# Three x tiles transposed by DMA instead of TensorE at the end of block 0, with one load and four small loads moved to other queues

## The chip, the cores and the metric

The kernel runs on one core of one Trainium2 chip. The metric is device time in microseconds (us), lower is better. The core's engines run side by side, each through its own list of instructions in program order: PE (TensorE, matrix products; its weight loads are shown apart as PEld), DVE (VectorE), ACT (ScalarE), POOL (GpSimd) and SP (SyncE). SP computes nothing here: it issues DMAs, and a DMA that it issues waits behind whatever SP issued before. All DMAs run on the core's 16 DMA engines. In the profile q1 is the queue of SP's DMAs and q0 that of the DMAs which POOL issues.

## What is computed

A linear attention with position weights, and behind it a gated feed-forward layer on its output. Cut to what matters:

```python
# q, k, v: (8 batches, 8 heads, 576 rows, 64) f32
phi(x) = concat([relu(x) * cos_w, relu(x) * sin_w], axis=-1)     # 64 -> 128
kv  = einsum('bhsf,bhsd->bhfd', phi(k), v);  z = sum_s phi(k)
out = einsum('bhsf,bhfd->bhsd', phi(q), kv) / (einsum('bhsf,bhf->bhs', phi(q), z) + 1e-6)
x   = out.transpose(0, 2, 1, 3).reshape(8 * 576, 512)
xn  = x / sqrt(mean(x * x, -1) + 1e-6) * rms_g
g   = xn @ w_gate                                                # 512 -> 1536
y   = (g * sigmoid(g) * (xn @ w_val)) @ w_out                    # 1536 -> 512
```

## The kernel before

The 4608 rows are worked in nine blocks of 512: blocks 0 to 7 are the first 512 rows of each batch, block 8 holds the last 64 rows of all eight batches (the tails). Blocks run in the order 0, 1, 2, 3, 4, 5, 6, 8, 7. A block has 12 steps of gate and value products (`gval_step`: four matmuls of 128x512 into a bank psG, four into a bank psV; then ACT makes the Silu of psG and DVE multiplies it with psV), and four steps of output products (`out_mm`, 12 matmuls each). psG and psV have two banks each, used in turn.

While PE works on block b, the attention of batch b+1 is made in its shadow. The order is written out by hand: `at(block, step, where, f, ...)` puts a call into a slot of a step, and the place of the call in the program is its place on each engine that it uses. In block 0 the steps 12 to 15 are pieces of the output products (`out_first`), with slots "pe", "mid", "pre" and "post". The pieces that matter here:

- `load_k`, `load_v`, `load_q` of a batch: 1 to 1.15 MB each from HBM into a ring of five tiles (`raw`). The loads of batch 2 are issued by POOL (G in the code) in the slots 8, 10 and 11 of block 0 (lines 714, 717 and 720); those of the later batches by SP.
- `q_phi` (DVE makes the cosine half, ACT the sine half) turns a quarter of a batch's q into bf16. For batch 2 the four quarters stand in steps 1 to 4 of block 1. Each is then transposed by a DMA of SP (`q_tr_dma`, line 320, tile qpT). The products with kv (`nd_pe`, line 417) read qpT: for batch 2 quarter 0 in step 6 of block 1, the others in steps 8, 10 and 12.
- `nd_post` and `x_sq` divide and square a tile of 128 rows of x; POOL makes the power -1/2 (line 488, `rs`); `x_norm` on DVE makes the bf16 tile `xn` (line 495).
- A tile `xn` (128 rows, 512 columns) is transposed into `xnT`, from which the matmuls of its block read. There are two ways. `x_tr` has PE make four transposes of 128x128 into a bank psV (line 514), and ACT (even tiles) or DVE (odd tiles) copies the bank to xnT (lines 277 and 279). `x_tr_dma` has SP issue one DMA that transposes the tile from one place of the on-chip memory to another (line 508). Before the change batch 1 uses `x_tr` for all four tiles, batches 2 to 7 use `x_tr_dma`.
- The first matmul of block 1 (line 524) needs all four tiles of batch 1.
- `load_q_tails` loads the last 64 rows of q of two batches by two DMAs of 128 KB (tile rqt, line 134), issued by SP. They are read in step 3 of a later block: the pair of batches 2 and 3 in block 2, the pair of batches 0 and 1 in block 3.
- The outputs of block 0 are copied from the banks by ACT and DVE (`osb`) and stored by four DMAs of SP (line 558).

`X1` names, for each of the four x tiles of batch 1, the slot of its products, of its norm and of its transposition:

```python
    X1 = (
        ((12, "mid"), (13, "pe"), (14, "pe")),
        ((13, "pe"), (13, "mid"), (14, "mid")),
        ((13, "mid"), (14, "pe"), (15, "pe")),
        ((14, "pe"), (14, "mid"), (15, "mid")),
    )
```

Of the kernel before, what the change touches and what calls it, by code (L numbers as in the profile page):

```python
# [17 lines left out]
def kernel(  # L18
# [11 lines left out]
    nc = tc.nc  # L30
# [16 lines left out]
    V, A, G = nc.vector, nc.scalar, nc.gpsimd  # L47
# [12 lines left out]
    psV = [ps.tile([P, 512], FP32, name=f"psV{i}") for i in range(2)]  # L60
# [67 lines left out]

    rqt = {}

    def load_q_tails(pair):
        rqt[pair] = two.tile([P, H, D], FP32, name="rqt", tag="rqt")
        for i in range(2):
            nc.sync.dma_start(
                out=rqt[pair][64 * i : 64 * i + 64, :, :],
                in_=q[2 * pair + i, :, 512:576, :].rearrange("h s d -> s h d"),
            )
# [558 lines left out]
    def at(blk, n, where, f, *args):  # L696
        slots.setdefault((blk, n), {}).setdefault(where, []).append((f, args))
# [19 lines left out]
    at(0, 10, "post", load_kv, "v", 2, (0, HP), G)  # L717
    at(0, 12, "pe", kvz_pe, 1)
    at(0, 12, "pe", kvz_evac, A, 1)
    at(0, 11, "post", load_q, 2, (0, 4), G)  # L720

    def x_tr(b, j, bank):
        x_tr_pe(b, j, bank)
# [3 lines left out]
# [6 lines that stand above are left out]
# [3 lines left out]
        if j:  # L736
            at(0, *X1[j - 1][1], x_norm, 1, j - 1)
    at(0, *X1[3][1], x_norm, 1, 3)
    for j in range(4):
        at(0, *X1[j][2], x_tr, 1, j, psV[j % 2])  # L740
    for nb in range(2, B):
        b = nb - 1
        first = nb == 2
# [24 lines left out]
    for pair in range(4):  # L768
        b = 2 * pair or 3
        if pair == 0:  # L770
            at(1, 15, "post", load_q_tails, 0)
        at(b, 3, "post", q_tails_phi, V, pair, 0)
        at(b, 3, "post", q_tails_phi, A, pair, 1)
        at(b, 3, "post", q_tails_tr_dma, pair)
        at(b, 12, "pe", nd_tails_pe, pair)
        at(b, 12, "pre", nd_post, 2 * pair + 1, 4)
        at(b, 12, "post", x_sq, 2 * pair + 1, 4)
        at(b, 13, "post", x_norm, 2 * pair + 1, 4)
        at(b, 13, "post", x_tr_dma, 2 * pair + 1, 4)
    for nb in range(3, B):  # L780
        b = nb - 2
        late = b == 1
        at(b, 0, "post", load_kv, "k", nb)
        at(b, 5 if late else 3, "post", load_kv, "v", nb)
        at(b, 8 if late else 6, "post", load_q, nb)
        if nb % 2 == 1:
            at(b, 9, "post", load_q_tails, nb // 2)

    def gval_step(blk, n):
        run(blk, n, "pe")  # L790
# [86 lines left out]
```

## Time and profile before

| what | value |
|---|---|
| median of 3 runs | 325.4 us (324.87 to 326.1) |
| the profiled execution | 325.76 us, of which the span from first to last instruction is 324.0 us |
| PE busy | 317.4 us (98% of the span) |
| PEld, DVE, ACT, POOL busy | 163.7, 184.3, 165.2, 40.7 us |
| granted TensorE clock | 1.000 over the span |
| DMA | 53.37 MB, 165 GB/s mean; q1 57.0% and q0 16.5% of 16 engines' span |
| SP's x transposes (line 508, 24 of them for xnT) | 1.19 / 1.22 / 3.83 us to issue (least, median, most) |

Times inside the span are counted from its start. A row of the timeline has the start, the length, the engine, the line and operation, the output and input, and, in brackets, the idle time before it with what ended it. Matmul ends are modelled: the distance from one start to the next tells what a matmul costs on PE, here 0.216 us for one of 512 columns. "us to landing" is the time from a DMA's issue until its data are there.

### The profile page before, as it was taken

What the parts mean: (1) busy time and instruction counts of PE and PEld (TensorE: products, weight loads), DVE (VectorE), ACT (ScalarE), POOL (GpSimd) and SP (SyncE); (2) the same over time, 40 slices, a digit from 0 to 9 for tenths busy, and PEclk for the clock granted to TensorE, in tenths of its full rate; (3) what the DMA queues carried; (4) which work ended last, traced back from release to release, by engine and by line L of the source; (5) the groups of instructions that cost most, each with busy time, mean ns of one, the idle gap of its engine ahead of it and who ended that gap; (6) DMA issues with size and microseconds to landing.
All of it is one profiled execution on the core that took longest, in us unless ns stands there. A gap on an engine that the chain in (4) does not pass through costs nothing.

```text
span 324.0 us, 6128 instructions
## 1 busy us (share of the span) xinstructions
PE 317.4 (98%) x2348; PEld 163.7 (51%) x2348; DVE 184.3 (57%) x379; ACT 165.2 (51%) x319; POOL 40.7 (13%) x78
## 2 busy tenths in 40 slices
PE   7989999999999999999999999999999999999996
PEld 3679665544454445444454445444544444444444
DVE  7784858757727774576557745782577034204410
ACT  5664856754574547445754575446643343223321
POOL 9771212001000110011001000110011000000000
PEclk9999999999999999999999999999999999999999
DMA  7999995999579966998699958995822300041002
GB/s 228 231 266 273 281 327 212 228 204 259 125 178 216 231 193 159 200 229 210 171 205 214 211 149 182 223 200 144 134 49 41 123 32 0 2 98 32 2 32 97
DMA packets 77627, 53.37 MB, mean 165 GB/s; under 512 B 50410, under 2 KB 71326, under 8 KB 77598
## 3 DMA queue, kind: packets, MB, share of 16 engines
q1 hardware_dynamic: 70374, 39.81, 57.0%
q0 software_dynamic: 7216, 13.17, 16.5%
q8 instruction: 18, 0.29, 0.4%
q14 instruction: 11, 0.09, 0.1%
q10 hardware_dynamic: 8, 0.00, 0.0%
HBM read 37.83 MB, written 9.44 MB: 146 GB/s over the span
## 4 chain that ended last, share of the span: by engine, by line
PE 92%; DMA 5%; POOL 2%; issue 0%; DVE 0%; POOLq 0%
PE psC L547 27%; PE psG L524 27%; PE psV L524 27%; DMA wv<-in_moe_w_val_dram 5%; PE psA L417 2%; PE psG L547 2%; PE psA L361 2%; PE psV L611 2%; PE psG L611 1%; PE psA L368 1%; POOL raw L124 1%; PE psA L442 0%; POOL wg L174 0%; POOL vv L204 0%; PE psC L337 0%; PE psV L514 0%
## 5 line engine op out<-in xcount | busy, mean ns | idle before, releaser
L544 DVE TENSOR_TENSOR hT<-psV,sg 128x512 bf16<-128x512 f32 x100 | 68.9, 689 | 102.2 <-PE psV L524 65.9
L543 ACT ACTIVATE sg<-psG 128x512 f32<-128x512 f32 x100 | 59.2, 592 | 63.2 <-PE psG L524 63.2
L524 PE MATMUL psV<-xnT,wv 128*128 128x512 bf16 x352 | 90.3, 379 | 0.0
L524 PE MATMUL psG<-xnT,wg 128*128 128x512 bf16 x352 | 90.3, 379 | 0.0
L547 PE MATMUL psC<-wo,hT 128*128 128x512 bf16 (+1 forms) x408 | 89.1, 376 | 0.0
L547 PEld LDWEIGHTS <-hT 128*128 128x128 bf16 x456 | 42.8, 98 | 47.1
L524 PEld LDWEIGHTS <-wv 128*128 128x128 bf16 x400 | 39.1, 98 | 47.2
L524 PEld LDWEIGHTS <-wg 128*128 128x128 bf16 x400 | 37.1, 98 | 39.7
L488 POOL TENSOR_TENSOR rs<-ms,mhalf 128x1 f32<-128x1 f32 x36 | 19.8, 551 | 195.9 <-ACT scr L483 195.9
L277 ACT COPY osb<-psC 128x512 f32<-128x512 f32 x32 | 18.8, 586 | 50.0 <-PE psC L547 50.0
L483 ACT ACTIVATE scr<-xt 128x513 bf16<-128x513 f32 x36 | 22.8, 634 | 24.5 <-DVE xt L467 24.5
L495 DVE SCALAR_TENSOR_TENSOR xn<-xt,rs,gb 128x512 bf16<-128x512 f32 (+1 forms) x37 | 26.9, 730 | 9.7 <-POOL rs L488 9.7
L283 ACT ACTIVATE kp<-raw,tab 128x256 bf16<-128x256 f32 (+2 forms) x50 | 28.4, 609 | 2.5 <-DMA raw<-in_k_dram 2.5
L467 DVE TENSOR_TENSOR xt<-psA,rec 128x512 f32<-128x512 f32 x36 | 24.9, 691 | 1.2
L283 ACT ACTIVATE qp<-raw,tab 128x512 bf16<-128x512 f32 x32 | 22.6, 713 | 1.1 <-DMA raw<-in_q_dram 1.0
L285 DVE TENSOR_SCALAR kp<-raw,tab 128x256 bf16<-128x256 f32 (+2 forms) x54 | 20.3, 421 | 0.7 <-DMA raw<-in_k_dram 0.7
L285 DVE TENSOR_SCALAR qp<-raw,tab 128x512 bf16<-128x512 f32 x31 | 15.3, 498 | 1.6 <-DMA raw<-in_q_dram 1.6
L417 PEld LDWEIGHTS <-qpT 128*128 128x128 bf16 x224 | 10.5, 97 | 6.6 <-issue 0.5
L524 PE MATMUL psG<-xnT_tail,wg 128*128 128x512 bf16 x48 | 12.3, 379 | 0.0
L524 PE MATMUL psV<-xnT_tail,wv 128*128 128x512 bf16 x48 | 12.3, 379 | 0.0
L417 PE MATMUL psA<-kvzs,qpT 128*128 128x65 bf16 x224 | 11.4, 193 | 0.0
L279 DVE CAST vv<-raw 116x1280 bf16<-116x1280 f32 (+1 forms) x13 | 10.5, 805 | 0.0
(95 smaller groups left out, 181.0 us busy)
## 6 DMA issues: line engine op xcount, KB each, us to landing
out_dram<-osb SPq DMA_DIRECT2D x31, 256.0 KB, 2.4
raw<-in_k_dram SPq DMA_DIRECT2D x5, 1120.0 KB, 8.1
raw<-in_v_dram SPq DMA_DIRECT2D x5, 1120.0 KB, 7.7
raw<-in_q_dram SPq DMA_DIRECT2D x5, 1024.0 KB, 9.0
raw<-in_k_dram POOLq DMA_DIRECT2D x2, 1152.0 KB, 19.5
raw<-in_v_dram POOLq DMA_DIRECT2D x2, 1152.0 KB, 15.9
raw<-in_q_dram POOLq DMA_DIRECT2D x2, 1024.0 KB, 16.0
wg<-in_moe_w_gate_dram POOLq DMA_DIRECT2D x3, 512.0 KB, 14.7
```

Of the source, the lines that this page charges most:

```text
L277: A.copy(out=o, in_=i)
L283: A.activation(out=out_ap, in_=in_ap, func=AF.Relu, scale=scale)
L285: eng.tensor_scalar(out=out_ap, in0=in_ap, scalar1=scale, scalar2=0.0, op0=ALU.mult, op1=ALU.max)
L417: nc.tensor.matmul(heads[:, g, hp, :], lhsT=qpT[:, h, j * P : (j + 1) * P], rhs=kvzs[b][:, g, hp * E : (hp + 1) * E], start=True, stop=True,)
L467: V.tensor_tensor(out=xt[:, 0:DM].rearrange("p (hp g d) -> p g hp d", g=2, d=D), in0=heads[:, :, :, 0:D], in1=rec[:, :, :].unsqueeze(3).to ...
L483: A.activation(out=scr[:, :], in_=xt[:, 0 : DM + 1], func=AF.Square, scale=1.0 / math.sqrt(DM), accum_out=ms[:, :],)
L488: G.tensor_tensor(out=rs[:, :], in0=ms[:, :], in1=mhalf[:, :], op=ALU.pow)
L495: V.scalar_tensor_tensor(out=xn_of[(b, j)][:, c], in0=x_of[(b, j)][:, c], scalar=rs_of[(b, j)][:, :], in1=gb[:, c], op0=ALU.mult, op1=ALU. ...
L524: nc.tensor.matmul(bank[:, cols[0] : cols[1]], lhsT=w[:, t, n * P : (n + 1) * P], rhs=x[:, t, cols[0] : cols[1]], start=(t == 0), stop=(t ...
L543: A.activation(out=sg[:, :], in_=g[:, 0:TB], func=AF.Silu)
L544: V.tensor_tensor(out=hT[:, n, :], in0=v[:, 0:TB], in1=sg[:, :], op=ALU.mult)
L547: nc.tensor.matmul(bank[:, 0 : cols[1] - cols[0]], lhsT=hT[:, n, j * P : (j + 1) * P], rhs=wo[:, n, cols[0] : cols[1]], start=(n == 0), st ...
```

## The change

In block 0, the tiles 0, 1 and 2 of batch 1 are transposed by `x_tr_dma` instead of `x_tr`, in the slot of their norm (one step earlier than before); tile 3 stays on PE and its copy on DVE. The load of q of batch 2 leaves POOL and slot (0, 11) and goes to SP, behind the three transposes, in slot (0, 14). `load_q_tails` gets the issuing engine as an argument: the pair of batches 0 and 1 and the pair of batches 2 and 3 are now loaded by POOL, in the same slots as before; the other two pairs stay with SP.

```diff
-    def load_q_tails(pair):
+    def load_q_tails(pair, eng=nc.sync):
         rqt[pair] = two.tile([P, H, D], FP32, name="rqt", tag="rqt")
         for i in range(2):
-            nc.sync.dma_start(
+            eng.dma_start(
...
-    at(0, 11, "post", load_q, 2, (0, 4), G)
...
-    for j in range(4):
-        at(0, *X1[j][2], x_tr, 1, j, psV[j % 2])
+    for j in range(3):
+        at(0, *X1[j][1], x_tr_dma, 1, j)
+    at(0, *X1[3][2], x_tr, 1, 3, psV[1])
+    at(0, *X1[3][1], load_q, 2)
...
-            at(1, 15, "post", load_q_tails, 0)
+            at(1, 15, "post", load_q_tails, 0, G)
...
-            at(b, 9, "post", load_q_tails, nb // 2)
+            at(b, 9, "post", load_q_tails, nb // 2, G if nb == 3 else nc.sync)
```

SP's list after its first two loads was: four stores of block 0, the two DMAs of k of batch 3, four transposes of q of batch 2. It becomes: three transposes of x, q of batch 2, the four stores, k of batch 3, the four transposes of q.

## The prediction

> **What bounds the kernel now.** I read the chain of waits first. Its share by engine, and three of its pieces around the changed place (start, length, engine, bank and line, matmuls):
>
> ```profile
> PE 92%; DMA 5%; POOL 2%; issue 0%; DVE 0%; POOLq 0%
> ...
> 54.23 0.86 PE psG L547 x4
> 55.75 1.29 PE psC L547 x6
> 57.04 0.86 PE psG L524 x4
> ```
>
> The DMA's 5% is one wait, for a weight that lands at 24.4 us. From there the pieces of PE follow each other to the end: the kernel is bound by PE's list of matmuls. So a change pays only by what it takes off that list, and costs only where PE has to wait. Next, PE's own timeline where the removed transposes stand:
>
> ```profile
> 52.33 0.39 PE L514 MATMUL psV<-ident,xn 128*128 128x128 bf16 x4
> 52.55 0.59 PE L547 MATMUL psC<-wo,hT 128*128 128x512 bf16 x2
> 52.98 1.03 PE L547 MATMUL psG<-wo,hT 128*128 128x512 bf16 x4
> 53.84 0.39 PE L514 MATMUL psV<-ident,xn 128*128 128x128 bf16 x4
> 54.07 1.03 PE L547 MATMUL psG<-wo,hT 128*128 128x512 bf16 x4
> 54.93 0.59 PE L547 MATMUL psC<-wo,hT 128*128 128x512 bf16 x2
> 55.36 0.39 PE L514 MATMUL psV<-ident,xn 128*128 128x128 bf16 x4
> 55.59 1.46 PE L547 MATMUL psC<-wo,hT 128*128 128x512 bf16 x6
> 56.88 0.59 PE L524 MATMUL psG<-xnT,wg 128*128 128x512 bf16 x2
> ```
>
> Read the starts, not the lengths: four transposes take 52.55 - 52.33 = 0.22 us of PE, and the six matmuls after the last take 1.29 us, 0.215 each, with no gap. Block 1 begins at 56.88. Then DVE at the same place:
>
> ```profile
> 53.71 0.75 DVE L495 SCALAR_TENSOR_TENSOR xn<-xt,rs,gb 128x512 bf16<-128x512 f32 x1 [0.84 <-POOL rs L488]
> 54.38 0.42 DVE L279 COPY xnT<-psV 128x512 bf16<-128x512 bf16 x1
> 54.72 0.87 DVE L285 TENSOR_SCALAR kp<-raw,tab 128x256 bf16<-128x256 f32 x3
> 55.50 0.68 DVE L279 COPY osb<-psG 128x512 f32<-128x512 f32 x1
> 56.10 0.41 DVE L279 COPY xnT<-psV 128x512 bf16<-128x512 bf16 x1
> ```
>
> Last, SP's queue, and how long its transposes of x take:
>
> ```profile
> 54.66 3.48 SPq L558 DMA_DIRECT2D out_dram<-osb  x4
> 58.25 1.01 SPq L115 DMA_DIRECT2D raw<-in_k_dram  x2
> 62.44 7.17 SPq L320 DMA_TRANSPOSE qpT<-qp  x4
> ...
> 86.38 1.24 SPq L508 DMA_TRANSPOSE xnT<-xn  x1
> ```
>
> ```profile
> DMA to landing us min/median/max: 2.5/7.7/9.5
> ```
>
> SP issues nothing between its first loads and 54.66.
>
> **Part 1: three transposes leave PE.** Twelve 128x128 transposes at 52.33/4 and its like: 0.22 + 0.22 + 0.23 = 0.67 us off PE's list. Two ACT copies of 0.57 and one DVE copy of 0.42 go too; they are in shadow.
>
> The fourth tile stays on PE and DVE, and now it is late. Its norm starts at 53.71 whatever PE does, since it waits for POOL's rs. DVE then goes on without the 54.38 copy: k work at 54.38, osb copy 0.78 later at 55.16, the xnT copy 0.60 later at 55.76, done at 56.17. PE without the three transposes would begin block 1 at 56.88 - 0.67 = 56.21. From the end of a DVE result to the waiting engine the trace has 0.09 (xt 46.91, ACT 47.00), and from the block's first weight load to its first matmul 56.88 - 56.67 = 0.21: so 56.17 + 0.30 = 56.47. Of the 0.67 a wait takes 0.26, and 0.41 is left. If the handover is hidden, 0.67 is left; I take 0.41.
>
> **Part 2: do the three DMA tiles land by then?** Each is issued when its norm ends: 49.48, 51.17, 52.87, at 1.2 us apiece, so SP is free again for the next each time; the last is issued from 52.9 to 54.1. Their price is bounded by two rows of line 508: 2.5 us at least, 7.7 in the median. The median belongs to transposes issued behind 1 MB loads on the same queue (105.2 us behind v, for one). The one at 86.38 has only a store ahead of it: in windows of half a microsecond its packets (under 512 B) run from 87.4 to 88.3, 1.9 us after the issue. Here nothing of SP's is ahead, so I take 2.5: the third tile is there at 55.4, before 56.47. With 7.7 it would be 60.6. POOL's queue is still moving v and k of batch 2 then:
>
> ```profile
> 49.00:52.00 3.00, 3.00 (x31) 1.65 (x29) 2.86 (x8) 1.38 (x4) 1.10 (x2) 1.00 1.00 353
> 52.00:55.00 3.00, 3.00 (x22) 1.59 (x20) 2.16 (x6) 2.15 (x6) 0.55 (x1) 1.00 0.23 78
> 55.00:59.00 4.00, 4.00 (x23) 1.92 (x22) 3.43 (x10) 3.66 (x10) 0.00 (x0) 1.00 0.65 226
> 59.00:62.00 3.00, 3.00 (x15) 1.27 (x13) 3.00 (x8) 2.66 (x6) 0.00 (x0) 1.00 0.89 170
> ```
>
> (busy time of PE, PEld, DVE, ACT, POOL, then clock, DMA share, GB/s). The share drops to 0.23 after 52, and q of batch 2, the last MB in that queue, is gone from it: tiles 0 and 1 may share with v, tile 2 has the DMA engines nearly alone. [...]
>
> **Part 3: q of batch 2 goes from 40.2 us on POOL to 54.1 us on SP.** First user: ACT's q work at 60.96, DVE's at 61.80, now 0.41 earlier, 60.55. The q load of batch 3 (issued 75.27) shows first data 1.8 us later and 3.2 us of data at 350 GB/s. So q2 is there at about 59.1 + 0.5. Cover: 0.9 us. If it were as late as the 9.0 us median landing of SP's q loads, 63.1, ACT and DVE would hold the Silu and product of step 2 by 2.6 us; PE needs psG back at 65.16 - 0.41 and would get it at about 64.4: still hidden, barely.
>
> What is late next are the DMAs behind it on the queue: the stores (3.0 us of DMA time, 55.0 to 59.4), k of batch 3 (its packets run 59.5 to 66.0, slow until 62), then the first q transpose, whose 1,024 small packets are through at 67.0; with 0.4 to arrive, 67.4. PE reads it at 68.61 (`nd_pe`, step 6). Slack 1.2, after part 1 0.8. After the change: q2 data to 58.6 to 59.1, stores to 61.6 to 62.1, k3 for 4.0 us (928 packets at 230 per us, its rate after 62) or for 6.5 as before: 65.6 to 68.6 against 66.0. So the transpose lands at 67.0 to 70.0, needed at 68.2: a wait of 0 to 1.8. [...]
>
> The stores' osb buffers are next needed at 82.7, k3 at 82.4: covered. SP also lets each DMA wait for the eighth before it; all those are long done.
>
> **Part 4: four tail loads go to POOL.** POOL's DMAs take 0.74 to 0.89 us each to issue; two in a row, 1.8 us, in step 9 and step 15. Next behind them on POOL is the rs of step 10, 3.4 us after that of step 8: covered. Readers are at 98.3 and 132.0, loads at about 79 and 94: covered by 19 us or more. It takes 1.44 and 1.30 us off SP, where transposes with slack follow: nothing. Without its cover a POOL issue would hold one norm by 1.8 us.
>
> **The sum** against the profiled execution's 325.76: -0.67 + 0.26 + 0.0 to 0.1 = about -0.4, 325.4. That execution lies 0.36 above the median of the runs, so 325.4 - 0.4 = 325.0.
>
> **Rivals.**
> (a) An x tile is late for block 1. Decides once the third lands after 56.3; with the 7.7 us median PE waits 60.6 - 56.2 = 4.4 instead of 0.26: net +3.7, 329.1. For it: POOL's queue has the engines full until 51.5, and most x transposes of the trace take so long. Against: those stood behind SP loads.
> (b) The first q transpose of batch 2 is late for `nd_pe` because the MB of q2 stands before k3. Decides from a landing after 68.2; at 70.0 it costs 1.8: 326.8. For it: only 0.8 us of slack. Against: the DMA engines idle at 52 to 57 now, which q2 fills.
> (c) q2 lands after 64 and DVE and ACT hold PE's banks: from there each us is lost, some 2: 327.0. Against: no SP load in the trace with an empty queue ahead.
> (d) The fourth tile eats the whole gain, or the DMA tiles land at 56.5: 325.4.
>
> **How the numbers follow.** Chances: forecast 0.55, (a) 0.15, (b) 0.18, (c) 0.04, (d) 0.08. The time is the likeliest, 325.0. Low end: 325.4 - 0.67 = 324.7, less 0.4 of scatter between runs, 324.3. High end: (b) at its dear end and the near part of (a), 327.2. About 0.5% (1.6 us) is what a measurement of this kernel can tell from no change. Faster by that needs more than PE has to give here: 0.04, scatter alone. Slower: most of (a) 0.12, some of (b) 0.03, (c) 0.03: 0.18. The rest, 0.78, is within.
>
> **What would show it.** PE: twelve transposes fewer, block 1 beginning at about 56.5 with a wait for DVE's copy; a wait for SP's DMA there means (a). `nd_pe` of step 6 without a gap; a gap means (b). ACT's first q work of batch 2 near 60.5 without idle time; if not, (c). The largest doubt is how small packets fare beside a queue of large ones.

## The result, and the profile after

| | before | changed |
|---|---|---|
| median of the runs, us | 325.42 (324.87 to 326.19) | 330.16 (327.1 to 331.97) |
| ratio to before | | 1.0129, 95% interval 1.0098 to 1.016 |
| profiled execution, us (its span) | 325.76 (324.0) | 327.28 (325.5) |
| granted clock of the profiled execution | 1.000 | 1.000 |

The change makes the kernel 1.3% slower; the forecast was 325.0, its range ended at 327.2. The profiled execution is one of the quickest of the changed kernel, 2.9 us under the median, so its profile holds only a part of the loss. More of it is in the profile of the first experiment. Medians here and below are over all runs; the ratios leave out the six runs that lie over 1.5% above the fastest of their kernel (one of f5, two of g2, three of g4).

The chain of waits of the changed kernel, its shares by engine and the pieces around the changed place (start, length, what):

```profile
PE 89%; DMA 8%; POOL 2%; issue 1%; DVE 0%; POOLq 0%
...
56.00 0.90 PE psG L524 x4
...
61.44 8.71 DMA qpT<-qp
70.14 0.05 issue
70.19 0.42 PE psA L417 x8
70.61 0.86 PE psG L524 x4
```

Before, the chain went from matmul to matmul here. Now a DMA stands in it: the first q transpose of batch 2, issued at 61.44, there at 70.15. The chain follows it over its whole 8.71 us; what PE loses is in PE's own timeline. First the products of step 6 before the change, then PE after it:

```profile
68.61 0.41 PE L417 MATMUL psA<-kvzs,qpT 128*128 128x65 bf16 x8
```

```profile
54.32 0.39 PE L514 MATMUL psV<-ident,xn 128*128 128x128 bf16 x4
54.55 1.46 PE L547 MATMUL psC<-wo,hT 128*128 128x512 bf16 x6
55.87 1.04 PE L524 MATMUL psG<-xnT,wg 128*128 128x512 bf16 x4
...
66.75 1.03 PE L524 MATMUL psV<-xnT,wv 128*128 128x512 bf16 x4
70.19 0.42 PE L417 MATMUL psA<-kvzs,qpT 128*128 128x65 bf16 x8 [2.41 <-DMA qpT<-qp]
```

Block 1 begins at 55.87 (before: 56.88), with one group of four transposes left on PE instead of four. `nd_pe` of step 6 begins at 70.19 (before: 68.61) after 2.41 us of idle time. Counted by starts it is 2.58, since the four matmuls from 66.75 were through at 66.75 + 4 x 0.216 = 67.61 (ends are modelled). This execution was already 0.37 ahead of the one of before at 40 us, for reasons outside the change: PE's wait for a weight ended at 24.07 instead of 24.45. So part 1 gave 56.88 - 55.87 - 0.37 = 0.64, and the wait took 2.58.

DVE and the weight loads at block 1's start:

```profile
55.40 0.41 DVE L279 COPY xnT<-psV 128x512 bf16<-128x512 bf16 x1
```

```profile
55.87 0.55 PEld L524 LDWEIGHTS <-wg 128*128 128x128 bf16 x4 [0.36 <-DVE xnT L279]
```

DVE's copy of the fourth tile is indeed the last thing to come, at 55.81, and the weight load waits for it. But PE's matmuls lose nearly nothing: the six matmuls from 54.55 take 1.29 us, to 55.84, and the next begins at 55.87.

SP's queue:

```profile
53.84 0.51 SPq L124 DMA_DIRECT2D raw<-in_q_dram  x1
...
57.38 0.45 SPq L115 DMA_DIRECT2D raw<-in_k_dram  x1
...
61.44 2.22 SPq L320 DMA_TRANSPOSE qpT<-qp  x1
```

The three x tiles landed 3.0, 2.5 and 2.4 us after their issue, the last at 54.9. q of batch 2 landed at 60.3 (6.5 us), 0.3 too late for ACT, which costs PE nothing. Its packets ran from 55.0 to 59.9, most of them before 59.5. The packets of k of batch 3 are those between 512 B and 2 KB in the DMA view of two windows, 928 in each: before from 59.45 to 66.20, after from 61.70 to 68.10.

```profile
DMA packets 1394, 1.32 MB, mean 196 GB/s; under 512 B 462, under 2 KB 1390, under 8 KB 1393
DMA packets 1508, 1.64 MB, mean 256 GB/s; under 512 B 413, under 2 KB 1341, under 8 KB 1507
```

So k took 6.7 us of packets before and 6.3 after. The first q transpose landed 2.1 us after its last packet.

### The profile page after: what moved, and what is told of

It is laid out like the page before. It is cut to its first block, busy times and chain, and to the rows that moved or that the text cites. A ratio compares the mean times of both kernels' runs of the same rounds, so it can differ in the third digit from the quotient of the medians.

```text
span 325.5 us, 6075 instructions
## 1 busy us (share of the span) xinstructions
PE 315.0 (97%) x2300; PEld 162.7 (50%) x2336; DVE 184.7 (57%) x378; ACT 164.2 (50%) x317; POOL 42.6 (13%) x81
## 4 chain that ended last, share of the span: by engine, by line
PE 89%; DMA 8%; POOL 2%; issue 1%; DVE 0%; POOLq 0%
PE psC L547 27%; PE psV L524 26%; PE psG L524 25%; DMA wv<-in_moe_w_val_dram 5%; DMA qpT<-qp 3%; PE psA L417 2%; PE psG L547 2%; PE psA L361 2%; PE psV L611 2%; PE psG L611 1%; POOL raw L124 1%; PE psA L442 0%; PE psA L368 0%; POOL vv L204 0%; POOL wg L174 0%
## 5 line engine op out<-in xcount | busy, mean ns | idle before, releaser
L543 ACT ACTIVATE sg<-psG 128x512 f32<-128x512 f32 x100 | 59.1, 591 | 66.1 <-PE psG L524 56.8
L524 PE MATMUL psG<-xnT,wg 128*128 128x512 bf16 x337 | 88.6, 379 | 0.7 <-issue 0.2
```

What stands on the lines that cost most here:

```text
L524: nc.tensor.matmul(bank[:, cols[0] : cols[1]], lhsT=w[:, t, n * P : (n + 1) * P], rhs=x[:, t, cols[0] : cols[1]], start=(t == 0), stop=(t ...
L543: A.activation(out=sg[:, :], in_=g[:, 0:TB], func=AF.Silu)
```

## The experiments

Every kernel ran beside the kernel before on the same chip; "over" is the median less that of before beside it.

| label | what it is | median, us (least to most) | over | ratio, 95% interval |
|---|---|---|---|---|
| e1_same_again | the changed kernel | 329.36 (326.87-330.06) | 3.85 | 1.0109 (1.0079-1.014) |
| e2_q2_on_gpsimd | changed, q of batch 2 on POOL as before | 326.05 (325.53-326.6) | 0.54 | 1.002 (1.0008-1.0032) |
| e3_k3_behind_two | changed, k of batch 3 two steps later | 329.78 (329.43-329.98) | 4.27 | 1.0137 (1.0122-1.0153) |
| e4_q2_alone | before, q of batch 2 on SP | 326.43 (325.68-327.2) | 0.92 | 1.003 (1.0018-1.0043) |
| f1_q2_behind_store | the same, in a later slot | 329.22 (328.6-329.58) | 4.03 | 1.0129 (1.0114-1.0144) |
| f2_x_alone | before, three x tiles by DMA | 326.27 (325.86-326.94) | 1.08 | 1.0035 (1.0023-1.0047) |
| f5_k3_behind_two_q2_gpsimd | e2 and e3 together | 330.27 (327.33-335.27) | 5.08 | 1.0135 (1.0094-1.0175) |
| f7_filler_in_wait | changed, ten matmuls in the wait | 328.0 (327.65-328.88) | 2.81 | 1.0087 (1.0074-1.0101) |
| g1_k3_on_gpsimd | changed, k of batch 3 on POOL | 329.53 (327.77-330.5) | 3.74 | 1.0117 (1.0091-1.0142) |
| g2_k3_q2_on_gpsimd | e2 and g1 together | 326.65 (324.8-331.45) | 0.86 | 1.0029 (0.9992-1.0066) |
| g3_tails_alone | before, the tails on POOL | 325.91 (325.29-326.21) | 0.12 | 1.0007 (0.9997-1.0017) |
| g4_no_late_fourth_tile | g2, fourth tile copied by ACT | 327.36 (324.67-331.5) | 1.57 | 1.0028 (0.9995-1.0061) |
| h1_k3_after_x | g2, k held until the x tiles are there | 325.62 (325.07-326.23) | 0.18 | 1.0005 (0.9993-1.0016) |
| h2_no_late_fourth_tile | h1, fourth tile copied by ACT | 325.57 (324.84-326.11) | 0.13 | 0.9997 (0.9987-1.0008) |
| h4_x_alone_q2_early | f2, q of batch 2 on SP, early | 326.93 (326.01-327.7) | 1.49 | 1.0043 (1.0027-1.006) |
| k1_x_alone_24_back | f2, twelve small matmuls at the start | 326.09 (325.11-327.38) | 0.71 | 1.0018 (1.0005-1.0032) |
| k2_no_late_24_back | h2, the same twelve | 325.26 (324.72-326.4) | -0.12 | 0.9996 (0.9985-1.0008) |
| k3_after_24_back | changed, the same twelve | 328.43 (326.74-329.79) | 3.05 | 1.0087 (1.0058-1.0116) |

### What the wait costs: e1 and f7

> The changed kernel as it is, for more executions and a second profile. Theory Q (the MB of q of batch 2 stands before k of batch 3 on SyncE's queue, so the first q transpose of batch 2 lands about 70 us and PE waits for it) expects a wait of 2 to 5 us at the products of step 6 of block 1 in every profile, with block 1 itself beginning on time (55.9 to 56.5). It expects the executions near 330 us to be those where that wait is long enough that the granted clock falls behind it: a clock under 1.00 in the stage after the wait, and 1.00 before. Rival X (an x tile lands late for block 1 in those executions) expects a wait of PE at the start of block 1 in a profile of a long execution, and the clock to fall there. Rival C (this kernel's time scatters with the chip whatever its DMAs do) expects the kernel before to scatter as much in the same call.

No x tile was late and the kernel before scattered only from 324.8 to 326.1 beside it, so rivals X and C fall away; the wait and the clock are as expected. The 12 runs of the changed kernel, the first six and these, fall into two groups: four at 326.9 to 327.4 with a mean clock of 0.999 to 1.000, and eight at 329.3 to 332.0 with 0.99 to 0.995. The profile of e1 (329.4 us) is of the second. The windows of e1 around the wait (busy time and instructions of PE, PEld, DVE, ACT and POOL, then granted clock, DMA share, GB/s):

```profile
68.00:70.00 2.00, 0.12 (x1) 0.00 (x0) 0.69 (x1) 0.00 (x0) 0.00 (x0) 1.00 0.86 87
70.00:70.50 0.50, 0.00 (x0) 0.00 (x0) 0.00 (x0) 0.00 (x0) 0.00 (x0) 0.78 1.28 282
70.50:71.00 0.50, 0.00 (x0) 0.00 (x0) 0.00 (x0) 0.00 (x0) 0.00 (x0) 0.50 1.28 291
71.00:72.00 1.00, 0.98 (x10) 0.71 (x11) 0.29 (x2) 0.00 (x0) 0.00 (x0) 0.50 1.25 272
72.00:73.00 1.00, 1.00 (x4) 0.31 (x3) 0.77 (x2) 0.00 (x0) 0.00 (x0) 0.50 0.97 189
...
73.50:74.00 0.50, 0.50 (x3) 0.25 (x2) 0.00 (x0) 0.50 (x2) 0.00 (x0) 0.80 1.01 115
```

and its chain of waits behind it:

```profile
71.64 1.71 PE psG L524 x4
73.34 1.10 PE psV L524 x4
74.44 0.86 PE psG L524 x4
```

PE waits 2.9 us for the transpose, and some 2.2 us into the wait the granted clock falls to half. It stays there until about 73.7, so the next matmuls take 1.71 and 1.10 us where they took 0.86. Between 71.02 and 74.44 that is 0.20 for `nd_pe` (0.62 against 0.42), 0.85 and 0.24: 1.29 us. With the wait, 0.49 longer than in the first profile, and a block 1 that began 0.34 later, it makes up the 2.1 us between the two spans. In the first profile 2.41 us passed without such a fall, and in k3 (below) 2.9:

```profile
68.00:70.00 2.00, 0.09 (x1) 0.00 (x0) 0.69 (x1) 0.00 (x0) 0.00 (x0) 1.00 0.94 85
70.00:70.50 0.50, 0.00 (x0) 0.00 (x0) 0.00 (x0) 0.00 (x0) 0.00 (x0) 1.00 1.28 283
70.50:71.00 0.50, 0.01 (x1) 0.01 (x1) 0.00 (x0) 0.00 (x0) 0.00 (x0) 1.00 1.28 290
```

So the length of the wait alone does not decide whether the clock falls, and what does is not shown. The 3.4 us at half clock that e1 shows make a mean of 0.995 over its run, which most of the second group have; the longest run (331.97, 0.99) would hold two, an estimate from that. There is no trace of a run of this kernel above 329.4.

f7 fills the idle time:

```diff
+        if first:
+            at(b, 6, "pe", filler, 10, psC[1])
```

> The changed kernel with ten matmuls of 512 columns on zeros (2.16 us on PE, result unused) put on PE's list right before the products of step 6 of block 1, where it waits. The q transpose lands when it did. Theory clock (the executions near 330 us are those in which the granted clock halves for 3 to 4 us behind the idle wait): PE is idle there for under 1 us, the clock stays at 1.00 in every execution and the times gather at 327.0 to 327.6, with none above 328.5. Rival: if the wait itself is longer in those executions, they stay near 329 to 330 with clock 1.00.

PE's timeline in f7:

```profile
67.58 2.32 PE L569 MATMUL psC<-warm 128*128 128x512 bf16 x10
71.78 0.42 PE L417 MATMUL psA<-kvzs,qpT 128*128 128x65 bf16 x8 [1.88 <-DMA qpT<-qp]
```

The clock is 0.999 to 1.000 in all five runs (before this edit in four of 12), and the runs from 329.3 up are gone. So in these runs the clock's fall went with the idle time. The median is 1.0 us less over than in e1, but the intervals of the two ratios overlap. All five runs lie above the 327.0 to 327.6 expected, one, of 328.88, far above: the transpose itself came at 71.7 in it. Its landing varies, 70.1 to 71.7 over the profiles of the changed kernel, f7 and k3.

### What makes the transpose late: e2, f1, f2, e4 and g3

```diff
# e2, against the changed kernel
+    at(0, 11, "post", load_q, 2, (0, 4), G)
-    at(0, *X1[3][1], load_q, 2)
```

> The changed kernel with the load of q of batch 2 given back to GpSimd in its old slot; three x tiles still by DMA, tails still by GpSimd. Theory Q: no wait at step 6 of block 1, clock 1.00 throughout, about 0.4 us under the kernel before (324.9 to 325.2). Rival X: the x transposes share the DMA engines with q of batch 2 until 54 us, so the wait at block 1 gets longer and the time stays at 327 or more. Rival T (the tail loads on GpSimd are what costs): the time stays at 327 or more with no wait at either place.

```diff
# f1, against the kernel before (e4: at(0, *X1[3][1], load_q, 2) in the same place)
-    at(0, 11, "post", load_q, 2, (0, 4), G)
+    at(0, 14, "post", load_q, 2)
```

> The kernel before with q of batch 2 on SyncE's queue right behind the first store of block 0 (its first store is ready at 54.7 us, so q cannot go out early as it did in the run with q alone). x tiles on PE, tails on SyncE. Theory Q (what counts is the work that SyncE's queue holds ahead of the first q transpose of batch 2: here q's 3.2 us, no x transposes): a wait at step 6 of 2 to 4 us, 327.5 to 331. Theory T (the x transposes are needed for the wait, since q alone showed none): no wait, 325.4 to 326.

> The kernel before with one edit only: q of batch 2 loaded by SyncE at the end of block 0 instead of by GpSimd. The x tiles stay on PE, the tails on SyncE. Theory Q: the whole loss without the gain: a wait of 2 to 5 us at step 6 of block 1, 327.5 to 333 us. Rival X and rival T: 325.4, as before.

With q of batch 2 taken back to POOL the wait at step 6 falls to 0.7 and the time to 0.54 over, not to none and 0.4 under as expected. With q alone put ahead of k on SP's queue, and all x tiles on PE, the wait is 2.4 again. The waits of PE in e2 and in f1 (engine and bank, what it waited for, us in all, times, longest):

```profile
PE psA L417 <- DMA qpT<-qp: 0.7, 1, 0.7
PE psA L417 <- DMA qpT<-qp: 2.4, 1, 2.4
```

One MB ahead of k is enough; the x tiles aren't needed for it. e4 was meant as this test and was not: with nothing else in SP's list ahead of it, the load was issued at 35.22, as soon as its buffer was free, and PE then waited 0.4 for a weight. There was no wait at step 6. Its profiled execution (325.68) is the quickest of ten; what the others lose has no trace.

```diff
# f2, against the kernel before
-    for j in range(4):
-        at(0, *X1[j][2], x_tr, 1, j, psV[j % 2])
+    for j in range(3):
+        at(0, *X1[j][1], x_tr_dma, 1, j)
+    at(0, *X1[3][2], x_tr, 1, 3, psV[1])
```

> The kernel before with the three x tiles by DMA and nothing else: q of batch 2 on GpSimd, all tails on SyncE. Against the run that gave q of batch 2 back to GpSimd this puts the two pairs of tails back too. If the tails on GpSimd cost nothing (my prediction): the same 326.0, with about 0.7 us of wait at step 6. If they cost something: under 325.8. If they help by leaving SyncE's queue: over 326.3.

```diff
# g3, against the kernel before
-            at(1, 15, "post", load_q_tails, 0)
+            at(1, 15, "post", load_q_tails, 0, G)
-            at(b, 9, "post", load_q_tails, nb // 2)
+            at(b, 9, "post", load_q_tails, nb // 2, G if nb == 3 else nc.sync)
```

> The kernel before with only the two pairs of q tails loaded by GpSimd. Predicted at nothing: 325.2 to 325.5, no wait, the rs of step 10 on time.

The tails cost nothing (1.0007, and no new wait). The x tiles alone, which should have gained, lose 1.08: PE waits 1.0 at step 6, though no MB was added to SP's queue. That is a second cause, taken up below. (The profiled execution of f2 is the slowest of its six; it also lost clock in its first 20 us, 0.90 to 0.93, outside the change.)

### Moving the lateness away: e3, f5, g1, g2 and g4

```diff
# e3 and f5
-        at(b, 0, "post", load_kv, "k", nb)
+        at(b, 2 if late else 0, "post", load_kv, "k", nb)
# g1, g2 and g4
-        at(b, 0, "post", load_kv, "k", nb)
+        at(b, 0, "post", load_kv, "k", nb, (0, HP), G if late else nc.sync)
# f5, g2 and g4 too: q of batch 2 on POOL, as in e2
# g4 too, in x_tr
-        x_tr_evac(V if j % 2 else A, b, j, bank)
+        x_tr_evac(A, b, j, bank)
```

> The changed kernel with the load of k of batch 3 moved from step 0 to step 2 of block 1, behind the first two q transposes of batch 2 on SyncE's queue; q of batch 2 stays on SyncE. Theory Q: the first transpose has only q and four stores ahead of it, lands at about 64 us, no wait at step 6, clock 1.00: 324.8 to 325.3. If the third transpose, now behind k, is late for step 10 (75 us), a small wait there. Rival X and rival T: no change against the changed kernel, 327 to 332.

> The changed kernel with q of batch 2 given back to GpSimd and k of batch 3 behind the first two q transposes of batch 2. Theory Q: no wait at step 6 (no k ahead of the transpose), and SyncE's queue carries 3 us less than in the run with k moved alone, so the last x tile of batch 2 lands before block 2 needs it: 0.67 less 0.26 less than the kernel before, 325.1. If the queue is still too full, the wait comes back at the start of block 2: 326 or more.

> The changed kernel with k of batch 3 loaded by GpSimd instead of SyncE, in the same slot; q of batch 2 stays on SyncE. GpSimd has nothing queued there, so k can go out at about 54 us beside q. Theory Q (one queue in order: what stands ahead of the first q transpose on SyncE's queue decides): q and the stores are through at about 62 to 63, the transpose lands at 65 to 67, no wait at step 6, clock 1.00: 324.8 to 325.3, unless a load then lands late somewhere else. Rival E (the 16 engines' total work decides, whichever queue it stands in): q, stores and k are through at 67 as before, the transpose lands at 69 to 71 and the wait stays, 326.5 to 330.

> The run before this one with q of batch 2 on GpSimd as well: SyncE's queue holds only the x transposes and the stores ahead of the first q transpose. Theory Q: no wait at step 6, lands under 66, and the gain of part 1 is left: 0.4 us under the kernel before, 324.7 to 325.1. Rival E: the wait of 0.7 us that the run with q on GpSimd showed stays: 326.0.

> As the run with k and q on GpSimd, and the fourth x tile copied from its bank by ACT instead of DVE. Part 1 says that DVE's copy holds block 1 back by 0.26 us; if so, PE begins block 1 0.2 to 0.3 us earlier against its own last matmul of block 0, the weight load's wait of 0.4 for that copy goes, and the time is 0.2 to 0.3 us lower than in that run. If ACT's copy is as late, the same time.

In all five the wait at step 6 is gone, and another has come in the trace; only half of g2's and some of g4's runs come near the time that theory Q gave. Waits of PE in e3:

```profile
PE psG L524 <- DMA xnT<-xn: 2.6, 1, 2.6
```

waits of PE in g1, from 60 to 80 us:

```profile
PE psG L524 <- ACT sg L543: 3.2, 1, 3.2
```

and PE's timeline in g2, in its slowest run:

```profile
60.98 0.58 PE L524 MATMUL psG<-xnT,wg 128*128 128x512 bf16 x1 [4.25 <-DMA xnT<-xn]
```

In e3 and f5 k runs later and the last x tile of batch 2 behind it is late for block 2 (in f5 by 7.7 us in a run of 335). In g1 the loads of k, on POOL's queue, and of q, on SP's, share the DMA engines: q landed 12.4 us after its issue, at 66.2, and ACT and DVE held PE's banks, which is the prediction's rival (c). In g2 k runs beside the third x tile, which landed 7.15 us after its issue and held block 1, which is rival (a); but only sometimes: six of g2's 12 runs took 324.8 to 325.4, six 327.9 to 331.5, and g4 is split likewise (its trace, of 327.3, has the same wait with 2.3). The quick six have a median 0.9 under that of before beside them; no trace of one was kept, so what they gain is not shown. The split also hides what g4's copy by ACT is worth. Between 50 and 92 us, what was taken from one transfer's place was missed at the next deadline in all five traces, by 2.6 us in e3, 7.7 in f5, 3.2 in g1, 4.25 in g2 and 2.3 in g4.

### The second cause: h1, h2, h4 and k1 to k3

```diff
# h1, against g2: a copy on POOL that reads the third x tile, ahead of the load of k
+    def wait_x():
+        G.tensor_copy(out=dum[:, :], in_=xnT[1][:, 0, 2 * P : 2 * P + 1])
+    at(1, 0, "post", wait_x)
# h2: h1, and x_tr's copy by ACT as in g4
# h4: f2 with q of batch 2 on SP, early
-    at(0, 11, "post", load_q, 2, (0, 4), G)
+    at(0, 11, "post", load_q, 2)
```

> The kernel of g2 (q of batch 2 and k of batch 3 both by GpSimd, so that SyncE's queue has neither), with one GpSimd copy of a single column of the third x tile of batch 1 put ahead of the load of k of batch 3, so that this load is issued only when the x tiles have landed, at about 55.5 us. Theory (the first q transpose is late because the MB of q stands ahead of it on SyncE's queue, and the x tile was late in g2 because the load of k lay beside it): no wait of PE at block 1's start beyond 0.4 for the fourth tile and none at step 6, the clock 1.000 in all runs, and a time of 0.3 to 0.6 under the kernel before, without the second group of g2 (327.9 to 331.5). Rival (a MB on GpSimd's queue delays a transpose on SyncE's just as one on SyncE's own does): a wait of PE for qpT of 1 us or more at step 6, and 326.5 or more.

> The kernel of h1 with the fourth x tile copied from PSUM by ScalarE instead of VectorE. If VectorE's late copy costs the 0.26 us that the prediction took from part 1, this is 0.2 to 0.3 us under h1 and PE has no wait for xnT at block 1's start. If the handover was hidden all along, or ScalarE is as late there, it equals h1 within 0.1.

> The three x tiles transposed by the DMA, all tails on SyncE as before, and q of batch 2 on SyncE but issued at about 35 us (ahead of the x tiles, as in e4), so that GpSimd's queue ends with v of batch 2, before the x transposes. It tells what made the first q transpose 1.0 us late in f2 (x alone). If it was sharing with the end of q of batch 2 on GpSimd's queue (one DMA engine behind the others): no wait of PE for qpT at step 6, and a time of about 0.4 under e4's 326.4 to 326.6 by the same call's kernel before, some 326.0. If it is the x transposes on SyncE's queue themselves: a wait of about 1 us at step 6 and 327.0 or more.

h1 removes the second group of g2 and ends level with the kernel before, not 0.3 to 0.6 under it: PE still waits 1.1 at step 6 (h2: 0.8), with neither k nor q on SP's queue. h4 still waits 0.8, with q of batch 2 issued at 35 us and so out of the way of x tiles and q transposes alike. In h1 and h2 the load of k runs on POOL's queue beside the transpose, so h1's rival keeps its wait but not its time; k2 below has the same load in the same place and no wait. So the wait of f2 has a cause besides the two loads. The windows of f2 (columns as above):

```profile
66.50:67.00 0.50, 0.50 (x4) 0.22 (x3) 0.09 (x1) 0.50 (x2) 0.00 (x0) 1.00 0.51 80
67.00:67.50 0.50, 0.50 (x4) 0.20 (x2) 0.50 (x1) 0.18 (x1) 0.00 (x0) 1.00 5.81 178
67.50:68.00 0.50, 0.50 (x4) 0.26 (x3) 0.49 (x2) 0.30 (x1) 0.00 (x0) 1.00 0.01 1
68.00:68.50 0.50, 0.50 (x3) 0.03 (x1) 0.00 (x0) 0.30 (x1) 0.00 (x0) 1.00 0.09 9
68.50:69.00 0.50, 0.03 (x1) 0.00 (x0) 0.36 (x1) 0.00 (x0) 0.00 (x0) 1.00 0.64 139
```

Amid the transposes the packets stand still for a microsecond, at 1 and 9 GB/s, where they move 272 to 292 in the windows of e1, k1 and k3. The DMA share of 5.81 there counts whole packets by their start: those begun there stayed open. Just before, in f2's DMA view of 66.25 to 66.5 (queue, packets, MB, share):

```profile
q8 instruction: 1, 0.02, 42.3%
```

By the name of its queue this is a load of instructions, one packet of 16 KB; the pages of before and of the changed kernel have 18 of them. In the kernel before the same one begins between 64.25 and 64.5, ahead of most of the transposes' packets, and no stretch stands still. In all 20 traces of before, the changed kernel and the experiments, between 48 and 115 us, there are 49 stretches in which a quarter of a microsecond has a share above 3 and the next half at most 20 packets; 47 of them begin within 2 us after an instruction load began. The kernel before has none, though it has the loads: not every load is followed by one.

The theory tested next was that such a load comes when PE has taken a certain number of instructions, 1,487 to 1,491 matmuls and weight loads in before, f2, e2 and e4. Part 1 took 24 off (twelve transposes and their weight loads), so the load would come 24 instructions later in the work. In f2 and e2 it does. k1 to k3 put 24 back at a place where PE waits anyway:

```diff
     filler(10, psC[1])
+    for _ in range(12):
+        nc.tensor.matmul(
+            psC[1][:, 0:64], lhsT=warm[:, 0:P], rhs=warm[:, 0:64], start=True, stop=True
+        )
```

> The kernel of f2 (the three x tiles by the DMA and nothing else of the change) with twelve matmuls of 64 columns on constants added among the first warm-up matmuls, where PE waits 0.7 us at 4.9 us; their result is not used. They put back the 24 PE instructions (12 matmuls, 12 weight loads) that part 1 took off PE's list. Theory: in every trace a 16 KB load of instructions comes by a queue of its own when PE has issued about 1,490 instructions; in the kernel before at 64.25 us, ahead of the first q transpose's packets, in f2 at 66.25, amid them, and they stand nearly still from 67.5 to 68.5. With the 24 instructions back the load is at about 64 us again, no PE wait for qpT at step 6 above 0.2, and the time is about 1 us under f2's: 0.2 to 0.6 below the kernel before of this call. Rival (the x transposes themselves hold the q transpose up, or GpSimd's queue does): a wait of 0.8 to 1.1 at step 6 as in f2 and 0.9 to 1.2 above the kernel before.

> The kernel of h2 (neither k of batch 3 nor q of batch 2 on SyncE's queue, k held until the x tiles have landed, the fourth tile copied by ScalarE) with the same twelve matmuls. Theory of the instruction load: h2's wait of 0.8 us at step 6 is gone and the time is 0.6 to 0.9 under h2's, 0.4 to 0.7 below the kernel before of this call. Rival (a transpose lands 7 us after its issue behind any MB): the wait stays at 0.8 and the time equals h2's.

> The changed kernel with the same twelve matmuls. If the instruction load, which came at 67.0 to 67.75 us amid the last packets of k of batch 3 and the first transpose's, is a part of the 2.4 to 2.9 us wait at step 6, the load moves to about 65 and the wait falls by 0.5 to 1.2 us, to 1.3 to 2.2, with a time of 326 to 327.5 and a clock nearer 1.000. If q of batch 2 ahead of k of batch 3 makes the whole wait, it stays at 2.4 or more and the time at 327 to 330.

In k1's DMA view the load is back between 64.5 and 64.75, and k1's windows show:

```profile
66.00:66.50 0.50, 0.50 (x5) 0.21 (x3) 0.00 (x0) 0.50 (x2) 0.00 (x0) 1.00 0.18 10
66.50:67.00 0.50, 0.50 (x4) 0.26 (x3) 0.46 (x1) 0.32 (x1) 0.00 (x0) 1.00 0.67 148
67.00:67.50 0.50, 0.50 (x4) 0.21 (x3) 0.50 (x2) 0.17 (x1) 0.00 (x0) 1.00 1.27 281
67.50:68.00 0.50, 0.50 (x5) 0.19 (x2) 0.13 (x1) 0.43 (x1) 0.00 (x0) 1.00 1.28 292
68.00:68.50 0.50, 0.50 (x11) 0.38 (x10) 0.23 (x1) 0.00 (x0) 0.00 (x0) 1.00 1.25 273
```

The pause is shorter and 1.5 us earlier, the transpose takes 6.0 us instead of 7.3, and `nd_pe` begins at 68.00 without a wait (f2: 69.51). k2 has none either, against h2's 0.8. So putting the 24 instructions back takes the wait away, twice out of two. That it does so by moving the load is not shown. Counted by weight loads, of which each trace has all, the load begins after 745 in before, 744 in f2 and 746 in e2. But it begins after 734 to 737 in e3, f5, g1, g2, g4 and h2 (740 in h1, 742 in h4), where the twelve are gone too: within four weight loads that is the old place in the work. And in k2 it begins no earlier than in h2, at 64.75 against 64.02 us. What differs there is how long its one packet takes. The load in h2 and in k2 (share of 16 engines in a quarter of a microsecond: 2.9 and 1.3 us):

```profile
q8 instruction: 1, 0.02, 71.4%
q8 instruction: 1, 0.02, 32.5%
```

In the five traces with this wait (e2, f2, h1, h2, h4) the packet ends at 66.9 to 68.0, amid the transposes' packets; in before, e4, g3, k1 and k2, without it, at 65.2 to 66.1. Whether the load holds up the transposes, or something else holds up both, the runs do not tell.

The totals follow only in part. k2 is 0.25 under h2 by "over", less than the 0.6 to 0.9 expected, and the two intervals overlap; k2's holds 1, so no version here is shown to beat the kernel before. k1 gains 0.37 on f2, again with overlapping intervals, and stays 0.71 over. Its trace shows a part of that at the start of block 1:

```profile
56.27 1.02 PE L524 MATMUL psG<-xnT,wg 128*128 128x512 bf16 x4 [0.25 <-DMA xnT<-xn]
```

The third x tile landed at 56.13, and by the starts PE lost 0.42 there. With q of batch 2 on POOL it lands at 54.3 to 55.1, beside the x tiles, and the third took 2.7 to 3.6 us in e2, f2, f5, h1, h2, k1 and k2, where the changed kernel has 2.4. What the slower runs of k1 lose has no trace and stays open.

In k3 the load did not come earlier: at 67.75, when PE had taken 1,528 instructions, and the wait is 2.9. In the changed kernel it starts while k's packets thin out, about 1 us before the last of them (67.1 in the first profile, 67.8 in e1), which fits a load that stands behind them, but that wasn't tried by itself. The branch that put the whole wait down to q ahead of k gave 2.4 or more and 327 to 330, and it holds.

## Why the prediction was wrong, step by step

- **Part 1, right in mechanism, mis-sized.** The twelve transposes went and the fourth tile came last, at the moment worked out: the copy was to end 0.71 before the old start of block 1, and ended 0.37 + 0.70 before it in an execution 0.37 ahead. But the handover, taken at 0.30, was 0.06, and the 0.26 taken from the gain was 0.03. The gain is 0.64. h1 and h2, which differ in nothing but the engine of that copy, agree within 0.05 in the median, but that decides little: in h2's trace PE waits for the third x tile instead, 0.40 by the starts.
- **Part 2, right.** 2.4 us to landing for the third tile against 2.5, with no load beside it, as the prediction gave for its reason. Rival (a) was real: g2 shows it as soon as a MB runs beside that tile.
- **Part 3, the step that failed.** The prediction gave a wait of 0 to 1.8, and its sum took 0.0 to 0.1 of it. No run shows that term: PE waited 2.41 us in the first profile and 2.90 in e1. The term that was mis-sized is k of batch 3: 4.0 us, "928 packets at 230 per us, its rate after 62". That rate was misread. Before the change it holds from 62 to 63 (234 packets), while 62 to 66 has 160 per us. After it k took 6.3 us, against 6.7 before. Why k is slow is not shown. q's data took 4.9 us instead of 3.2, and the transpose needed 2.1 us behind k's last packet where 1.4 was reckoned. It landed at 70.1, or 70.5 on the clock of the profile before, past the late end of 70.0, and PE needed it 0.2 earlier than reckoned because part 1 gave more. The wait was 2.4 to 2.9 by the traces (2.6 to 3.1 by starts), more than rival (b)'s 1.8. f1 shows that q ahead of k does this alone, e2 that without it 0.7 is left, which goes with the second cause (a still stretch at 66.75, 0.3 after an instruction load began).
- **Part 3, a term that was missing.** In e1 the clock fell to 0.50 in the wait of 2.9 us, and eight of 12 executions have a mean of 0.995 or less. It cost 1.29 us in e1. By starts the profiled run comes to -0.64 - 0.37 + 2.58 = +1.57 of the 1.58 by which step 6 is late. For e1: -0.64 + 3.07 + 1.29 = 3.72 of the 3.9 that its execution lies over before's median beside it. The runs of 330.5 to 332.0, which lift the first median to 330.2, are longer than this sum and have no trace.
- **Part 3, a second missing term.** In f2, h1, h2 and h4, with no MB added just ahead of the q transpose, its packets stand still after an instruction load, and PE waits 0.8 to 1.1. Putting 24 instructions back takes the wait away; by what path is open. In the changed kernel the wait for k covers it or includes it, and which of the two stays open too.
- **Part 4, right.** g3, the tails alone, is 0.12 over with an interval that holds 1, and has no new wait.
- **The chances.** Rival (b) was named with its place and its point of decision, at 0.18. It was priced from the landing alone, at 1.8, and slower by over 0.5% was given no more than 0.03 from it. That the kernel came out slower is not scatter: every one of its 12 runs lies above the kernel before's highest beside it, 326.2 and 326.1.

## What to carry to other kernels

Where a bulk load is moved onto a queue, work out the landing of the first small, urgent transfer behind it, take each load's rate over its whole length and not over its best microsecond, and if the slack is under a microsecond (0.8 was reckoned here) take the late end: here 1 MB ahead on such a queue cost some four us in the median (f1: 4.03). A wait can cost PE more than its length, here 1.29 us more in e1, where the granted clock fell to 0.50; with ten matmuls put into the wait it was 0.999 to 1.000 in all five runs of f7. And taking instructions from a list can cost elsewhere: with 24 fewer on PE's list f2 waited 1.0 us at step 6, with them back k1 did not. So look for instruction loads beside the next deadline before calling a removal free.

## What the runs showed of the hardware

- A DMA transpose that is under way can stop for about 1 us: 47 of 49 such stops, over the 20 traces, follow a load of instructions, one packet of 16 KB or 8 KB, within 2 us. That the load is the cause is likely, not shown. No wait goes with the load in the kernel before; in f2, h1, h2 and h4 one of 0.8 to 1.1 us does.
- The granted clock fell to 0.50 about 2.2 us into an idle stretch of PE in e1 and came back some 3.4 us later, 2.7 us after PE had work again. In k3 it stayed at 1.00 through an idle stretch of 2.9 us.
- A DMA transpose of one tile landed in 2.4 us with no load beside it, in 7.15 beside 1 MB on another queue (g2), and in 8.7 to 9.2 behind 2 MB of loads and 1 MB of stores on its own (the changed kernel, e1).
